# The first forty microseconds of a fused Fourier-and-mixer kernel written anew: other load order, other table order, other first rows

## The chip, the cores and the metric

The kernel runs on one core of a Trainium2 chip. The metric is the time of one execution on the device in microseconds (us); lower is better. The core has a matrix engine (PE, whose weight loads are shown as PEld), a vector engine (DVE), a scalar engine (ACT), a general engine (POOL) and an engine that mostly issues transfers (SP). Each works through its own list of instructions in order and waits on semaphores for the others. Transfers (DMA) are issued from SP, ACT or POOL and are carried by sixteen shared DMA engines.

## The reference

The input x has 8 batches of 3136 rows and 256 columns.

```python
X = np.fft.fft(x, axis=1)
X = np.fft.fft(X, axis=2)
x = X.real                              # what the mixer gets
xt = x.transpose(0, 2, 1)
h = xt @ U @ V                          # U: 3136 x 32, V: 32 x 3136
u = x + h.transpose(0, 2, 1)
ch = np.maximum(u @ w_ch1, 0.0) @ w_ch2 # 256 -> 1024 -> 256
out = u + ch
```

## The kernel before, in words

**The transform.** The Fourier transform over the rows is made by matrix products with tables of sines and cosines. The rows are folded first, so that symmetric and antisymmetric sums take the place of the rows themselves: x is loaded forward (`xf`, by indirect gathers on POOL, `load_f`) and backward (`xr`, by plain loads on SP, `load_r`; rows that stand alone by `load_0`). DVE makes even and odd sums along the columns (`along_d`, giving `EOF_` and `EOR_`; the two lone columns are copied by `alone` on POOL), then along the rows (`mirror`, giving `EOS`; `half`, giving `GE` and `GO`; `fourth`, giving `GC`). All of these DVE folds are recorded by one helper, line 422, so the profile tells them apart by their output: eor, eof, eos, ge, go, gc. PE multiplies them by the tables `TABE`, `TABO`, `TABS` (te, to, ts in the profile; `seq` and `even_rows`, output pt, all PE work through the helper at line 427). Results become `A` and `B`, halves of a spectrum over the rows, through copies on ACT and through `join` and `mirrored` on DVE. A second product with small column tables (`chan`, output pst) gives `S` and `T`, the rows that the mixer needs. A batch's `S` and `T` come in four pieces of 392 or 393 rows, each for S and for T.

**The low-rank part.** U goes through the same transform once, at the start (`transform_u`, output pu, line 295). Its result is written into spare columns of the tables, so that later products deliver the low-rank part along with the transform. `even_k` makes the even half, `odd_k` the odd half, `evict` copies both on ACT. For batch 0 the low-rank part is computed by itself (`u_alone`).

**The mixer.** 12,544 rows (half of each batch; the other half follows from symmetry) are worked through in 25 chunks of 512. `front(c, hf)` adds the low-rank part and stores `u`, then starts a transposing transfer `ut<-u` on SP. `direct` (p<-u,w) is the first mixer product of the direct half. `mirrors` adds a correction in place to get the mirrored half: p<-uo,wd with `WD`, the difference of the two halves of w_ch1, and p<-dv,qf with `DV`, differences of V. ACT applies the relu to both (h, lines 733 and 749). `second_product` (p<-w,h) multiplies by w_ch2, DVE adds `ut` (o, lines 792 and 793), POOL corrects two columns (`fx`), SP stores.

**What sets the order.** Everything up to `second_product(0, 0, 0)` is written out by hand in program order; each engine runs its share in that order. From there a loop over chunks places the later batches' transforms in slots (`due`, `put`, `spread_out`). Batch 1's folds are among the first of these slots; part of them stands in the hand-written beginning.

**The beginning.** The angles are made on DVE (`phase`), the tables on ACT (`sines`, `cosine_odd`, `other_odd` for odd-numbered tables; `sines`, `mirror_even`, `cosine_even`, `halve`, `other_even` for even ones). `negatives` are four small copies for U. `filler` issues products on PE whose result is not used. PSUM is shared by three tags: dft (two buffers), p1 (four) and p2 (two).

Places that matter: `VV` is V, loaded by POOL (line 904) and copied to three further groups of partitions by SP (line 939). `vv` gets one more column at line 960, `DV` is made at line 961, `WD` at 962, all three on DVE, and one row of `WD` is cleared on POOL. W2 is loaded on POOL at line 945, behind the gathers of batch 1's second half of `xf`.

Of the kernel before, what the change touches and what calls it, by code (L numbers as in the profile page):

```python
# [31 lines left out]
def kernel(  # L32
# [47 lines left out]

    def load_0(t, dst_f, dst_r, b, w):

        lo = t.offset + b * S * w
        nc.sync.dma_start(out=dst_f[PQ:KP],
                          in_=bass.AP(t.tensor, lo + (NI - 1) * w,
                                      [[w, 1], [784 * w, 4], [-w, NI], [1, w]]))
        nc.sync.dma_start(out=dst_r[PQ:KP, 0:3].rearrange("p q i d -> p q (i d)"),
                          in_=bass.AP(t.tensor, lo + 784 * w, [[w, 1], [784 * w, 3], [1, NI * w]]))
        nc.sync.dma_start(out=dst_r[PQ:KP, 3].rearrange("p i d -> p (i d)"),
                          in_=bass.AP(t.tensor, lo, [[w, 1], [1, NI * w]]))  # L90
# [35 lines left out]
    krow = gen.tile([P, 4 * NT], FP32, name="krow")  # L126
    kev = gen.tile([P, 2 * NT], FP32, name="kev")
    ncol = cpool.tile([P, NI], FP32, name="ncol")

    def iota(out_, pattern, base, m=0):  # L130
# [70 lines left out]
    def phase(y, a_ap, col_ap, bits):  # L201
# [3 lines left out]
        nc.vector.tensor_single_scalar(y, y, 2 ** bits - 1, op=AL.bitwise_and)  # L205

    def sine(out_, y, bits, sgn):
# [58 lines left out]
    hw = cpool.tile([P, 1], FP32, name="hw")  # L266
    nc.vector.tensor_scalar(hv[:], ncol[:, NI - 1:NI], 0.0, -0.5, op0=AL.is_equal, op1=AL.mult)
    nc.vector.tensor_scalar(hw[:], ncol[:, NI - 1:NI], 0.1245, -0.5, op0=AL.is_gt, op1=AL.mult)
    nc.vector.scalar_tensor_tensor(hv[:], hv[:], 1.0, hw[:], op0=AL.add, op1=AL.add)
    def kp(i):  # L270
# [19 lines left out]
    def transform_u(t, fill=None):  # L290
# [22 lines left out]
        def even_k():  # L313
            pu = PU[t] = psum.tile([P, 16, R], FP32, tag="p2", name="pu", bufs=2)
            for c, i in enumerate((3, 1)):
                for io in range(NI):
                    dst = pu[:kp(io), 2 * io + c, :]
                    if io % 2 == 0:
                        group(dst, [(wo(t, i, io, nm), go(i, nm)) for nm in range(2)])
                    else:  # L320
                        group(dst, [(we(t, i, io), gc(i, io))])
                fill(1)

        def odd_k():
            pu = PU[t]
            for nm in range(2):
                u = 1 - t if nm else t
                for io in (0, 2):
                    group(pu[:PQ, 8 + 2 * nm + io // 2, :],
                          [(wo(u, i, io, nn), go(i, nn, nm == 1 and (i == 2) == (nn == 0)))  # L330
                           for nn in range(2) for i in (0, 2)])
                for io in (1, 3):
                    group(pu[:kp(io), 12 + 2 * nm + io // 2, :],
                          [(we(u, i, io), gc(i, io, nm == 1 and i == 2)) for i in (0, 2)])
                fill(1)

# [59 lines left out]
    def alone(qs, src, dst, eng=None):  # L396

        (eng or nc.gpsimd.tensor_copy)(dst[:, qs, :, 128:257:128], src[:, qs, :, 0:129:128])
# [207 lines left out]
    def chan(b, ch, h, tag="dft"):  # L606
        d = ST[b]
        at, n0 = ((0, 0), (785, 1), (393, 786), (1177, 785))[ch]
        n = 393 if ch == 0 else 392
        pt = psum.tile([P, TE], FP32, tag=tag, name="pst", bufs=BUFS[tag])  # L610
# [22 lines left out]

    def transposed(b):

        pt = psum.tile([P, 2, P], FP32, tag="p2", name="ptd", bufs=BUFS["p2"])
# [4 lines left out]
        nc.scalar.copy(TD[b % 2][:], pt[:])  # L641

    def hidden(b, hh):

        pt = psum.tile([P, CH], FP32, tag="dft", name="pq", bufs=BUFS["dft"])
# [226 lines left out]
    for t in range(2):  # L872
        halve(t)
    for t in range(2):
        other_even(t)
    negatives()

    def filler(tag="dft"):
        pt = psum.tile([P, 2 * NT], FP32, tag=tag, name="fill", bufs=BUFS[tag])

        def some(n):
            for _ in range(n):
                nc.tensor.matmul(pt[:], TABO[0][:PQ, 0, 1, 0:P], TABO[0][:PQ, 0, 0, 0:2 * NT],  # L883
                                 start=True, stop=True)
        return some
# [17 lines left out]
    alone(EV, xf, EOF_)  # L903
    nc.gpsimd.dma_start(out=VV[:R, 0:S], in_=moe_V)
    gather(w1t[:], moe_w_ch1, D, pint[:], H, 0)
    alone(OD, xf, EOF_)
# [74 lines left out]
    mirrored(0, 1, cos_even)  # L981
    odd_part(0)

# [109 lines left out]
```

## Time and profile before

| What | us |
|---|---|
| Median of 3 runs (lowest, highest) | 465.75 (465.24, 467.85) |
| The profiled execution, and its span in the trace | 465.93, 464.1 |
| PE, DVE, ACT, POOL busy | 437.0, 319.3, 296.4, 124.3 |
| First sine on ACT starts | 3.50 |
| First gather of xf on POOL starts | 7.04 |
| First product of U's transform after the even tables | 19.48 |
| Granted TensorE clock at half | 19.15 to 32.80 |
| First channel product of batch 0 (pst) | 37.98 |
| First direct product of chunk 0 (p<-u,w) | 41.50 |
| First p<-dv,qf of chunk 0 | 49.55 |
| First second product (p<-w,h) | 54.89 |

How to read it: the span runs from the first to the last instruction of the one execution that was recorded. The chain of work that ended last is followed back from the last instruction, at each step to what released it. A line of the timeline has the start, the time from the first to the last end, engine, line, operation, output and inputs, and in brackets the idle time ahead and what ended it. A line of windows has the stretch, its length, the busy time (and instructions), the granted clock as a share of full speed, the mean share in which the DMA engines were busy, and GB/s.

### The profile page before, as it was taken

Reading aid. Unit: us, or ns where it says so; the run is one execution under the profiler, and the core shown is the slowest. Engines: PE = TensorE matmul, PEld = TensorE weight load, DVE = VectorE, ACT = ScalarE, POOL = GpSimd, SP = SyncE. Lnnn points to the kernel's source line nnn. Section 1 sums busy time; section 2 is a strip of 40 time slices with the busy share of each in tenths; the row PEclk is TensorE's granted clock in tenths of the full one; section 3 lists DMA queues with packets and bytes.
Section 4 is the critical chain, followed back from the end, with each engine's and each line's share of the span. In section 5 each row is a group of like instructions: output and inputs, shape, how many; then the busy total and the mean of one; then the engine's idle time right before and its main releaser. Section 6 shows DMA issues by size and latency. Waiting matters only on the chain.

```text
span 464.1 us, 8942 instructions
## 1 busy us (share of the span) xinstructions
PE 437.0 (94%) x3267; PEld 288.0 (62%) x3314; DVE 319.3 (69%) x649; ACT 296.4 (64%) x635; POOL 124.3 (27%) x340
## 2 busy tenths in 40 slices
PE   4897898997999999999999999999999999999995
PEld 1584366565756666666766666666666675666674
DVE  8886897787599596677686687768777544443542
ACT  6845655675557665777567756775576755766651
POOL 8651162313123230421233221241133100011010
PEclk9859999999999999999999999999999999999999
DMA  5899399597756947675859368565342532425463
GB/s 145 219 224 203 45 275 140 95 193 158 200 145 168 245 106 183 167 176 148 195 114 239 103 163 131 132 179 150 90 97 69 136 93 54 133 69 160 108 126 111
DMA packets 91231, 68.33 MB, mean 147 GB/s; under 512 B 57470, under 2 KB 84498, under 8 KB 91186
## 3 DMA queue, kind: packets, MB, share of 16 engines
q1 hardware_dynamic: 85714, 53.38, 50.8%
q0 software_dynamic: 5472, 14.36, 12.2%
q8 instruction: 26, 0.43, 0.4%
q14 instruction: 19, 0.16, 0.1%
HBM read 28.86 MB, written 25.69 MB: 118 GB/s over the span
## 4 chain that ended last, share of the span: by engine, by line
PE 82%; DVE 8%; ACT 6%; issue 2%; DMA 1%; DVEq 0%; POOL 0%; POOLq 0%
PE p L427 61%; PE pt L427 10%; PE pst L427 4%; PE ph L427 3%; DVE u L690 2%; PE pq L427 1%; PE pu L295 1%; ACT h L733 1%; PE fill L883 1%; DVE ge L422 1%; PE ptt L427 1%; DVE gc L422 1%; DMA ut<-u 1%; DVE A L582 1%; DVE o L792 1%
## 5 line engine op out<-in xcount | busy, mean ns | idle before, releaser
L427 PE MATMUL p<-w,h 128*128 128x256 bf16 x1576 | 188.6, 273 | 0.0
L427 PEld LDWEIGHTS <-h 128*128 128x128 bf16 x1576 | 149.9, 98 | 39.3 <-issue 16.5
L749 ACT ACTIVATE h<-p 128x512 bf16<-128x512 f32 (+1 forms) x200 | 101.5, 595 | 64.7 <-PE p L427 62.5
L733 ACT ACTIVATE h<-p 128x512 bf16<-128x512 f32 (+1 forms) x200 | 101.8, 601 | 8.9 <-PE p L427 8.8
L792 DVE TENSOR_TENSOR o<-p,ut 128x256 f32<-128x256 f32 x99 | 41.6, 420 | 94.8 <-PE p L427 72.8
L427 PE MATMUL p<-u,w 128*128 128x512 bf16 (+1 forms) x360 | 91.1, 374 | 3.6 <-DVE u L690 0.7
L797 POOL TENSOR_TENSOR o<-o,fx 128x2 f32<-128x2 f32 (+1 forms) x99 | 37.4, 379 | 136.5 <-issue 72.4
L427 PEld LDWEIGHTS <-w 128*128 128x128 bf16 x400 | 39.0, 98 | 40.6 <-issue 2.9
L427 PE MATMUL p<-uo,wd 128*128 128x512 bf16 (+1 forms) x199 | 50.7, 374 | 0.4
L57 POOL DMA_INDIRECT xf<-in_x_dram,xidx x32 | 37.0, 1155 | 18.4 <-issue 6.7
L793 DVE TENSOR_TENSOR o<-p,ut 128x256 f32<-128x256 f32 x99 | 40.9, 413 | 0.0
L422 DVE TENSOR_TENSOR eor<-xr 99x1016 bf16<-99x1016 f32 x32 | 38.3, 1209 | 3.5 <-DMA xr<-in_x_dram 3.5
L422 DVE TENSOR_TENSOR eof<-xf 99x1016 bf16<-99x1016 f32 x32 | 38.2, 1207 | 0.0
L690 DVE TENSOR_TENSOR u<-ph,T 128x512 bf16<-128x512 f32 (+8 forms) x64 | 35.0, 557 | 4.5 <-PE ph L427 2.8
L690 DVE TENSOR_TENSOR u<-ph,S 128x512 bf16<-128x512 f32 (+8 forms) x64 | 35.0, 557 | 1.8 <-PE ph L427 1.3
L706 POOL TENSOR_TENSOR fx<-ut 128x4 f32<-128x4 bf16 x50 | 12.8, 256 | 71.9 <-DMA ut<-u 71.9
L427 PEld LDWEIGHTS <-wd 128*128 128x128 bf16 x200 | 19.5, 97 | 17.1 <-issue 1.0
L427 PE MATMUL pt<-te,gc 98*128 98x229 bf16 (+1 forms) x192 | 24.6, 265 | 3.8 <-DVE u L690 3.6
L705 POOL TENSOR_TENSOR fx<-ut 128x4 f32<-128x4 bf16 x25 | 7.7, 306 | 75.3 <-DMA ut<-u 70.2
L427 PEld LDWEIGHTS <-go 98*128 98x128 bf16 x216 | 20.2, 101 | 8.8 <-issue 2.3
L427 PEld LDWEIGHTS <-gc 98*128 98x128 bf16 x216 | 19.9, 99 | 8.3 <-issue 4.0
L618 ACT CAST T<-pst 128x392 bf16<-128x392 f32 (+1 forms) x28 | 17.4, 621 | 11.5 <-PE pst L427 11.5
(154 smaller groups left out, 468.6 us busy)
## 6 DMA issues: line engine op xcount, KB each, us to landing
out_dram<-o SPq DMA_DIRECT2D x33, 512.0 KB
xr<-in_x_dram SPq DMA_DIRECT2D x14, 784.0 KB
out_dram<-o SPq DMA_DIRECT2D x8, 384.0 KB
out_dram<-o SPq DMA_DIRECT2D x9, 256.0 KB
xr<-in_x_dram SPq DMA_DIRECT2D x1, 1568.0 KB
out_dram<-o SPq DMA_DIRECT2D x8, 128.0 KB
ut<-u SPq DMA_TRANSPOSE x50
vv<-vv SPq DMA_DIRECT2D x3, 196.0 KB
```

Of the source, the lines that this page charges most:

```text
L57: nc.gpsimd.indirect_dma_start(out_, None, bass.AP(t.tensor, t.offset, [[w, rows], [1, w]]), bass.IndirectOffsetOnAxis(idx, 0), element_of ...
L422: ins = nc.vector.tensor_tensor(*a, **k)
L427: ins = nc.tensor.matmul(*a, **k)
L618: nc.scalar.copy(to, pt[:, :n])
L690: nc.vector.tensor_tensor(u[:, s, at:at + hi - lo], phs[s][:, at:at + hi - lo], src, op=AL.add)
L705: nc.gpsimd.tensor_tensor(fx[:, :, 0], ut[:, n:2 * n, 0], ut[:, 0:n, 0], op=AL.subtract)
L706: nc.gpsimd.tensor_tensor(fx[:, :, 1], ut[:, 0:n, 0] if hf else ut[:, n:2 * n, 0], ut[:, n + 1:2 * n + 1, 0], op=AL.subtract)
L733: nc.scalar.activation(k["h", 0][q][:, j - 4 * q, :w], p1[:, :w], AF.Relu)
L749: nc.scalar.activation(k["h", 1][q][:, g, :w], k["p1"][g][:, :w][:, ::-1], AF.Relu)
L792: nc.vector.tensor_tensor(o[:, ts, 0:P], p2[:, :w, 0:P], ut[:rows, ts, 0:P], op=AL.add)
L793: nc.vector.tensor_tensor(o[:, ts, P:D], p2[:, :w, P:D], strip(ut[:rows], (CH // P + t0 + 1) * P, [[P, w], [-1, P]]), op=AL.add)
L797: nc.gpsimd.tensor_tensor(o[:, ts, cols], o[:, ts, cols], fx[:rows, ts, 1 - hf:], op=AL.add)
```

## The change

- **Loads.** The three row loads of U are issued from ACT. On SP, `xr`'s odd half goes ahead of the row loads of x, the even half behind them. The four gathers of batch 0's `xf` move ahead of the clearing of the GO and GC buffers (`zeros`) on POOL, which goes behind the table code.
- **Tables.** `kev` is gone; the even angles are read from parts of `krow` in two instructions instead of one. The odd tables of both kinds are finished before the even ones begin; `negatives` moves ahead of the even cosines. The factor `hv` is made on POOL instead of DVE, with four instructions for three.
- **U's transform.** Both odd halves run first, then the even halves, then the copies. 24 fillers stand ahead, 12 between, 8 behind, where 40 stood ahead; `odd_k` has two fillers where it had one.
- **V and the weights.** V's load and the gather of w1t move ahead on POOL. W2's load moves ahead of the second half of batch 1's gathers. `WD`, the extra column of `VV` and `DV` are made on POOL.
- **Chunk 0's rows.** `first_rows` makes only the first 256 columns of pieces 0 and 1, and later the other 136. Piece 2 takes one more row (393), which piece 1 gave before. `transposed` and the two `hidden` products share one p2 buffer with fillers (`spare`), and pieces of batch 0's last rows use p2.
- **Order around chunk 0.** `odd_part(0)` goes ahead of the last `mirrored`; piece 3 moves behind `direct(0, 1)`; the folds of batch 1's backward rows move: the odd ones behind `front(0, 1)` and behind piece 3, the even ones behind `front(1, 0)`.

```diff
-    load_0(moe_U, UA, UR, 0, R)
+    load_0(moe_U, UA, UR, 0, R, nc.scalar)
     load_r(moe_U, UR, 0, 0, 4, R)
+    load_r(x, xr, 0, 1, 2, D)
     load_0(x, xf, xr, 0, D)
-    for q0 in (1, 0):
-        load_r(x, xr, 0, q0, 2, D)
+    load_r(x, xr, 0, 0, 2, D)
     iota(jv[:], [[1, KP]], 0, 1)
-    iota(kev[:, 0:NT], [[-2, 2], [-4, NT // 2]], 392)
-    iota(kev[:, NT:2 * NT], [[-2, NT]], 391)
+    for q in (0, 2, 1, 3):
+        load_f(x, xf, 0, q, D)
...
-    zeros(nc.gpsimd, 0)
-    zeros(nc.gpsimd, 1)
-    for q in (0, 2, 1, 3):
-        load_f(x, xf, 0, q, D)
...
+    def first_rows(b, at, tag):
+        d = ST[b]
+        n = 256 if at == 0 else 136
+        for h in range(2):
+            pt = psum.tile([P, 2, 256], FP32, tag=tag, name="psf", bufs=BUFS[tag])
+            for c, lo in enumerate((at, 785 + at)):
+                mm(pt[:, c, :n], MC[:, h * P:(h + 1) * P], d["A"][:, lo:lo + n], start=True, stop=False)
+                mm(pt[:, c, :n], MSN[:, h * P:(h + 1) * P], d["B"][:, lo:lo + n], start=False, stop=True)
+            to = strip(d["ST"[h]][:], 2 * at, [[1, 2], [2, n]])
+            if h == 1:
+                nc.vector.tensor_copy(to, pt[:, :, :n])
+            else:
+                nc.scalar.copy(to, pt[:, :, :n])
...
     flipped = flip_u()
-    for i in (3, 1):
-        phase(phe[:, i // 2], kev[:KP], ncol[:KP, i:i + 1], 15)
-        sines(i)
-        mirror_even(0, i)
-    fold_u(flipped)
-    for i in (3, 1):
-        cosine_even(i)
     for i in (0, 2):
         cosine_odd(i)
     for t in range(2):
         other_odd(t)
+    for i in (3, 1):
+        phase_even(i)
+        sines(i)
+        mirror_even(0, i)
+    fold_u(flipped)
+    negatives()
+    for i in (3, 1):
+        cosine_even(i)
+    halves()
+    zeros(nc.gpsimd, 0)
+    zeros(nc.gpsimd, 1)
     for t in range(2):
         halve(t)
     for t in range(2):
         other_even(t)
-    negatives()
...
     alone(OD, xr, EOR_)
+    nc.gpsimd.dma_start(out=VV[:R, 0:S], in_=moe_V)
+    gather(w1t[:], moe_w_ch1, D, pint[:], H, 0)
     alone(EV, xr, EOR_)
...
-    fill(40)
+    fill(24)
     us, uc = transform_u(0, fill), transform_u(1, fill)
-    for f in us + uc:
-        f()
+    us[1]()
+    uc[1]()
+    fill(12)
+    us[0]()
+    uc[0]()
+    us[2]()
+    uc[2]()
+    fill(8)
...
+    nc.gpsimd.dma_start(out=W2[:], in_=moe_w_ch2.rearrange("(j p) d -> p j d", p=P))
     for q in (1, 3):
         load_f(x, xf, 1, q, D)
-    nc.gpsimd.dma_start(out=W2[:], in_=moe_w_ch2.rearrange("(j p) d -> p j d", p=P))
...
     apart(0, 1, sin_odd)
+    nc.gpsimd.tensor_tensor(WD[:], W1[:, 1, :], W1[:, 0, :], op=AL.subtract)
+    nc.gpsimd.memset(WD[0:1], 0.0)
     nc.gpsimd.memset(DV[:, 0:1], 0.0)
-    nc.vector.tensor_copy(VV[2 * R:, S:S + 1], VV[2 * R:, HALF:HALF + 1])
-    nc.vector.tensor_tensor(DV[:, 1:], VV[:, S - 1:HALF:-1], VV[:, 1:HALF], op=AL.subtract)
-    nc.vector.tensor_tensor(WD[:], W1[:, 1, :], W1[:, 0, :], op=AL.subtract)
-    nc.gpsimd.memset(WD[0:1], 0.0)
+    nc.gpsimd.tensor_copy(VV[2 * R:, S:S + 1], VV[2 * R:, HALF:HALF + 1])
+    nc.gpsimd.tensor_tensor(DV[:, 1:], VV[:, S - 1:HALF:-1], VV[:, 1:HALF], op=AL.subtract)
...
-    join(0, 1, 0, sin_odd)
+    join(0, 1, 0, sin_odd, high=False)
     lowrank(0)
-    filler("p2")(6)
-    for ch in range(2):
-        for h in range(2):
-            chan(0, ch, h)
+    spare = psum.tile([P, CH], FP32, tag="p2", name="spare", bufs=BUFS["p2"])
+    transposed(0, spare)
+    filler("p2", spare)(6)
+    join(0, 1, 0, sin_odd, low=False)
+    first_rows(0, 0, "dft")
+    hidden(0, 0, spare)
...
-    alone(OD, xr, EOR_)
-    alone(EV, xr, EOR_)
     front(0, 0)
     mirrored(0, 0, sin_even)
     join(0, 1, 1, cos_odd, low=False)
+    odd_part(0)
     mirrored(0, 1, cos_even)
-    odd_part(0)
...
     direct(0, 0)
-    transposed(0)
-    along_d(OD, xr, EOR_, 0)
     chan(0, 2, 0)
     chan(0, 2, 1)
-    along_d(OD, xr, EOR_, 1)
-    hidden(0, 0)
-    hidden(0, 1)
-    chan(0, 3, 0)
-    chan(0, 3, 1)
+    hidden(0, 1, spare)
+    first_rows(0, 256, "p2")
     mirrors(0, 0)
     front(0, 1)
+    alone(OD, xr, EOR_)
+    along_d(OD, xr, EOR_, 0)
     direct(0, 1)
-    along_d(EV, xr, EOR_, 0)
-    mirrors(0, 1)
-    along_d(EV, xr, EOR_, 1)
-    front(1, 0)
+    chan(0, 3, 0, "p2")
+    chan(0, 3, 1, "p2")
+    along_d(OD, xr, EOR_, 1)
+    mirrors(0, 1)
+    front(1, 0)
+    alone(EV, xr, EOR_)
+    along_d(EV, xr, EOR_, 0)
+    along_d(EV, xr, EOR_, 1)
```

More of the change, by code (lines that the diff above doesn't have):

```diff
@@ L126 @@
     krow = gen.tile([P, 4 * NT], FP32, name="krow")
-    kev = gen.tile([P, 2 * NT], FP32, name="kev")
     ncol = cpool.tile([P, NI], FP32, name="ncol")
@@ L205, in phase, with phase_even @@
         nc.vector.tensor_single_scalar(y, y, 2 ** bits - 1, op=AL.bitwise_and)
+    def phase_even(i):
+        y, col = phe[:, i // 2], ncol[:KP, i:i + 1]
+        for part, src in ((slice(0, NT), strip(krow[:KP], NT // 2, [[NT, 2], [1, NT // 2]])),
+                          (slice(NT, 2 * NT), krow[:KP, 3 * NT:4 * NT])):
+            dst = y[:, part].bitcast(FP32)
+            if part.start == 0:
+                dst = dst.rearrange("p (a j) -> p a j", a=2)
+            nc.vector.tensor_scalar(dst, src, col, float(2 ** (23 - 15)), op0=AL.mult, op1=AL.add)
+        nc.vector.tensor_single_scalar(y, y, 2 ** 15 - 1, op=AL.bitwise_and)
     def sine(out_, y, bits, sgn):
@@ L266, with halves @@
     hw = cpool.tile([P, 1], FP32, name="hw")
-    nc.vector.tensor_scalar(hv[:], ncol[:, NI - 1:NI], 0.0, -0.5, op0=AL.is_equal, op1=AL.mult)
-    nc.vector.tensor_scalar(hw[:], ncol[:, NI - 1:NI], 0.1245, -0.5, op0=AL.is_gt, op1=AL.mult)
-    nc.vector.scalar_tensor_tensor(hv[:], hv[:], 1.0, hw[:], op0=AL.add, op1=AL.add)
+    def halves():
+        nc.gpsimd.tensor_scalar(hv[:], ncol[:, NI - 1:NI], 0.0, -0.5, op0=AL.is_equal, op1=AL.mult)
+        nc.gpsimd.tensor_scalar(hw[:], ncol[:, NI - 1:NI], 0.1245, -0.5, op0=AL.is_gt, op1=AL.mult)
+        nc.gpsimd.tensor_tensor(hv[:], hv[:], hw[:], op=AL.add)
+        nc.gpsimd.tensor_single_scalar(hv[:], hv[:], 1.0, op=AL.add)
     def kp(i):
@@ L313, in even_k @@
         def even_k():
-            pu = PU[t] = psum.tile([P, 16, R], FP32, tag="p2", name="pu", bufs=2)
+            pu = PU[t]
             for c, i in enumerate((3, 1)):
@@ L324, in odd_k @@
         def odd_k():
-            pu = PU[t]
+            pu = PU[t] = psum.tile([P, 16, R], FP32, tag="p2", name="pu", bufs=2)
             for nm in range(2):
@@ L334, in odd_k @@
                           [(we(u, i, io), gc(i, io, nm == 1 and i == 2)) for i in (0, 2)])
-                fill(1)
+                fill(2)
         def evict():
@@ L609, in chan @@
         n = 393 if ch == 0 else 392
+        if b == 0 and ch == 2:
+            at, n0, n = 392, 784, 393
         pt = psum.tile([P, TE], FP32, tag=tag, name="pst", bufs=BUFS[tag])
@@ L632, in lowrank, with transposed @@
         nc.sync.dma_start_transpose(out=TD[b % 2][:], in_=TX[:])
-    def transposed(b):
-        pt = psum.tile([P, 2, P], FP32, tag="p2", name="ptd", bufs=BUFS["p2"])
+    def first_rows(b, at, tag):
[11 more added lines that the diff above has]
+                nc.scalar.copy(to, pt[:, :, :n])
+    def transposed(b, spare):
+        pt = spare[:, 0:2 * P].rearrange("p (s m) -> p s m", s=2)
         for s in range(2):
@@ L640, in transposed, with hidden @@
                    stop=(typ == 1))
-        nc.scalar.copy(TD[b % 2][:], pt[:])
-    def hidden(b, hh):
-        pt = psum.tile([P, CH], FP32, tag="dft", name="pq", bufs=BUFS["dft"])
+        nc.scalar.copy(TD[b % 2][:], pt)
+    def hidden(b, hh, spare=None):
+        pt = spare or psum.tile([P, CH], FP32, tag="dft", name="pq", bufs=BUFS["dft"])
         for s in range(2):
@@ L875, with filler @@
         other_even(t)
-    negatives()
-    def filler(tag="dft"):
-        pt = psum.tile([P, 2 * NT], FP32, tag=tag, name="fill", bufs=BUFS[tag])
+    def filler(tag="dft", pt=None):
+        pt = pt or psum.tile([P, 2 * NT], FP32, tag=tag, name="fill", bufs=BUFS[tag])
         def some(n):
             for _ in range(n):
-                nc.tensor.matmul(pt[:], TABO[0][:PQ, 0, 1, 0:P], TABO[0][:PQ, 0, 0, 0:2 * NT],
+                nc.tensor.matmul(pt[:, 0:2 * NT], TABO[0][:PQ, 0, 1, 0:P], TABO[0][:PQ, 0, 0, 0:2 * NT],
                                  start=True, stop=True)
@@ L903 @@
     alone(EV, xf, EOF_)
-    nc.gpsimd.dma_start(out=VV[:R, 0:S], in_=moe_V)
-    gather(w1t[:], moe_w_ch1, D, pint[:], H, 0)
     alone(OD, xf, EOF_)
```

9 lines of the change are left out of this document (5 added, 4 removed).

## The prediction

> **What bounds the kernel now.** I read the page's slices first, then the clock by its windows, then the chain that ended last, then DVE's rows and the DMA queues of the first 72 us.
>
> ```profile
> PE   4897898997999999999999999999999999999995
> DVE  8886897787599596677686687768777544443542
> PEclk9859999999999999999999999999999999999999
> PE 82%; DVE 8%; ACT 6%; issue 2%; DMA 1%; DVEq 0%; POOL 0%; POOLq 0%
> ```
>
> A slice is 11.6 us. From about slice 6 on PE is at 9 nearly everywhere, and 82% of the chain is PE. The change leaves that stretch's work as it is, so what counts is when PE gets into it: the first second product (p<-w,h) starts at 54.89 us in the timeline. All before it is the beginning, in which slice 3 shows the clock at 5. In stretches of 3.41 us (columns: length, PE busy, granted clock, DMA share, GB/s):
>
> ```profile
> 15.73:19.15 3.42, 1.79 (x11) 1.00 0.84 219
> 19.15:22.56 3.41, 3.08 (x30) 0.50 0.60 124
> 29.39:32.80 3.41, 3.41 (x16) 0.50 1.02 250
> 32.80:36.21 3.41, 3.41 (x70) 1.00 1.03 234
> 43.04:46.45 3.41, 2.21 (x14) 1.00 1.43 138
> ```
>
> After a stretch of which PE was busy 1.79 us the clock halves, and it is whole again after a stretch full of long matmuls. A stretch with 2.21 us keeps it. The half-speed time covers U's transform and the first half of batch 0's.
>
> Between 55 and 71 us the chain runs through DVE, not PE:
>
> ```profile
> 56.31 3.15 DMA ut<-u
> 59.73 0.27 POOL eof L398
> 60.64 0.42 DVE o L792
> ...
> 68.04 1.14 DVE ge L422
> 69.43 1.30 DVE gc L422 x2
> 70.73 0.61 DVE u L690
> 71.38 0.56 PE pt L427 x4
> ```
>
> Here PE waits 1.1 us for DVE's u. So two dates decide: when DVE enters this list, and what the list holds. From 71.4 us to 98.9 us the chain is PE again, so a shift at 71.4 us is taken to the end.
>
> ```profile
> 50.93 0.68 DVE L690 TENSOR_TENSOR u<-ph,S 128x511 bf16<-128x511 f32 x1
> 51.52 2.33 DVE L422 TENSOR_TENSOR eor<-xr 99x1016 bf16<-99x1016 f32 x2
> 54.99 0.69 DVE L690 TENSOR_TENSOR u<-ph,S 128x512 bf16<-128x512 f32 x1 [1.13 <-PE ph L427]
> 60.02 0.70 DVE L422 TENSOR_TENSOR eos<-eof,eor 99x1040 bf16<-99x1040 bf16 x1 [0.55 <-POOL eof L398]
> ```
>
> The eor pair lies in a gap in which DVE waits for chunk 0's second direct product, and 1.13 us are still left over.
>
> **Part by part.**
>
> *Loads first.* In the timeline the first gather of xf starts at 7.04 us, behind memsets from 3.60 to 6.81, and xr's large loads at 5.63, behind three small ones. Now the gathers follow the iotas (about 2.6 us) and xr's odd half goes third (about 2). The row loads of U go to ACT's queue, where ACT sat idle until 3.50 (three issues of 0.42 to 0.82 fit; at worst its first sine is 0.5 us late). The x loads end about 2.5 us earlier, at 16.3 instead of 18.8. DVE's 1.52 us wait for xr at 14.85 goes. The memsets move behind the gathers and end near 12.6, before POOL's first cast, which stood at 12.30.
>
> *Tables.* hv leaves DVE (0.15 + 0.14 + 0.16); the even phases take three instructions for two, twice (+0.35). ACT's list keeps its length, so the even tables stay near 19.5 us, but the odd ones are ready near 11 (16.69 before). The odd half of U's transform then stands where PE had only fillers, and fillers cover the rest up to 19.5. I take the clock as whole from here on: the gap left before batch 0's first products is about 1.3 us, and gaps up to 1.11 us (at 70.27) did no harm, one of 1.9 us (17.6 to 19.5) did. At half speed this stage costs at most 3 us, but not at the end (below).
>
> *DVE up to the first rows.* Less 1.52 and 0.45, plus 0.35: the last quarter-length fold ends at 29.6 us, not 31.22. vv, dv and wd (0.15 + 0.98 + 0.68) and the 1.01 us wait for vv leave DVE, and the second eh waits no longer (0.99), since PE, no longer at half speed, is ahead of it. B's first half is then ready at 32.05 (37.32 before) and the channel products start at 32.6, not 37.98.
>
> *First rows alone.* Two pieces of 256 columns per half instead of two of 393 let the first direct product start after one round of evictions (0.60 on ACT and DVE beside each other) instead of two: 35.1 us instead of 41.50 with the above. The rest of chunk 0's rows, the two pq products and B's and A's mirrored halves (0.60 each on DVE, between) bring PE to mirrors(0,0)'s dv products at 40.5 us, against 49.55.
>
> *dv on POOL.* This decides. In the built program POOL's copy into VV, which stands ahead of the dv subtraction, first waits for the landing of all of batch 1's gathers of xf. On DVE it waited for VV's copies only. Before, the last two gathers start at 29.21 and 30.97:
>
> ```profile
> L57 POOL DMA_INDIRECT xf<-in_x_dram,xidx x2: 1457/1539/1621, 29.2 to 31.0; - x2
> DMA to landing us min/median/max: 12.9/12.9/12.9
> ```
>
> That is 42.1 to 43.9 us. Now W2's load (512 KB) is ahead of them on the same queue, so they are its last entry, as W2 was, whose packets end near 46.5. The queues are full from about 26 us to there (the DMA share is 1.02 to 1.22 in the stretches I read), so the end moves with the end of the x loads, by 2.5, to 44.0. Chunk 0's transposes, which took the DMA share to 2.30 at 44 us, now fall before that end: +0.5. I take 44.5; from 41 (the gathers keep their 12.9 us from 27.5 and 29) to 47 (the transposes cost 3).
>
> Then POOL's copy (0.2) and dv, 1567 columns with two inputs. No POOL row of that size exists. DVE takes 0.98 for it, the floor. POOL's one-row memset of 1024 bf16 took 0.94, so 1567 make 1.44 for one stream and 4.3 for three. [...] dv is there at 44.5 + 0.2 + 2.9 = 47.6 us: 1.95 earlier than 49.55, where PE could have had 9.05. If POOL is late, PE waits behind dv with front(0,1) and all after it, ACT with the second relu, and DVE with u.
>
> [...]
>
> *DVE's list behind dv.* The eor folds of batch 1's odd rows now follow u of front(0,1), with the S and T copies of the last channel piece between; they fill the gap that the even pair filled, and pass it by 0.4. The even pair (2.33) moves behind u of front(1,0), so it lies on the chain; it covers the 0.55 wait for POOL's eof. Net +0.4 + 2.33 - 0.55 = +2.2. Its cast (alone) and the transposes (3.15) are done in its shade.
>
> *The clock once more.* From 40.5 to 47.6 PE has nothing: over 3.4 us, so the clock halves, and front(0,1), eight direct products (0.22 each, then 0.43) and the correction run slow for one stretch or two. ACT's relus (0.51 each) hide part: eight at 0.43 are 3.4 against four relus of 0.51, 2.1. I take +1.0, from 0 to 1.7.
>
> *Free.* Banks: the spare tile shares ptd, fillers and both pq products; its order of writers is PE's own, and a conflict would cost an eviction (0.60) in a stretch where PE is early anyway. W2 earlier: its user stands at 52 us or later. Fewer early fillers: PE is idle otherwise. Queue order on SP is otherwise kept.
>
> **Sum.** -1.95 + 2.2 + 1.0 = +1.25 us. The profiled execution took 465.93 us (span 464.1), so 467.2; it lies 0.18 above the median of the runs, 465.75, so I predict 467.0.
>
> **Rivals.**
>
> *The gathers land early.* If they are down by 37 us, dv is ready at 40.5 and costs nothing. No clock loss: -9.05 + 2.2 = -6.8, 459 us. For it: every load starts earlier, and full overlap of POOL's wait was gained already at 37. Against: the queues have no free share before 46. Landings between give the times between; from 42 us on the gain is under 2.3. Chance of a time below 463.4 this way: 0.28.
>
> *The gathers land late.* With W2's small packets and the transposes both ahead, 47 us, and dv at 4.3: 51.5 us, that is +1.95 + 2.2 + 1.7 = +5.9, 471.6 us. It decides from a landing of about 45.5 on. For it: the last packets before trickled until 48. Chance 0.30.
>
> *The clock stays at half speed from 19 us.* The fillers between the small products might not count as busy: with one filler per six products in 19.15 to 32.80 the clock did not come back. Then the channel products start 3 us later and dv's turn on PE is 43.5: still before 47.6, so alone 467 stands; it only takes away the early landing's gain. Inside the other cases.
>
> *Forecast,* landing at 42 to 45.5: 463.4 to 468.1 us, chance 0.42.
>
> **Numbers.** A change within 0.5% (2.3 us) counts as none; the three runs spread by 2.6. Faster 0.28 (early landing), same 0.42, slower 0.30 (late). The range for 8 in 10 is 459.5 to 470.5; the likeliest case alone has 464 to 468.
>
> **What would show it.** In the trace after: POOL idle from about 34.5 us until the gathers land, then vv and dv of about 3 us; PE idle ahead of p<-dv near 47 us with POOL as releaser; the granted clock 1.00 from 12 to 40 us and 0.50 once behind 44; the first direct product near 35 us; DVE's even eor pair behind the third pair of u. I am wrong if p<-dv follows p<-uo at once near 40 us, if POOL's dv is far from 3 us, or if PE no longer waits for DVE near 71 us.

## The result, and the profile after

The changed kernel takes 468.13 us (median of 17 runs, 464.67 to 474.5), the kernel before 464.5 (17 runs beside it, 462.76 to 467.91). The ratio is 1.0064, with a 95% interval of 1.0036 to 1.0091: 3.0 us slower (1.7 to 4.2), against a forecast of 1.25. The ratio leaves out two executions of the changed kernel that were over 1.5% above its fastest. The profiled execution took 467.82 us with a span of 466.0, which is 1.9 over the one before.

What the new beginning was to give did not come: U's odd half runs early, but batch 0's rows come later than before. The dates, in us:

| | before | after | forecast |
|---|---|---|---|
| xr's even half is down | 16.37 | 19.52 | 14.85 or earlier |
| first product of U's transform | 17.55 | 12.34 | near 11 |
| first channel product | 37.98 | 40.38 | 32.6 |
| first direct product | 41.50 | 42.96 | 35.1 |
| PE is through p<-uo,wd, next is p<-dv | 49.5 | 48.5 | 40.5 |
| first p<-dv | 49.55 | 49.54 | 47.6 |
| batch 1's first pt | 71.38 | 74.62 | |

DVE's timeline after (start, length, engine, line, operation; in brackets the idle time ahead and what ended it) shows where it begins:

```profile
11.38 2.36 DVE L434 TENSOR_TENSOR eor<-xr 99x1016 bf16<-99x1016 f32 x2
19.52 2.35 DVE L434 TENSOR_TENSOR eor<-xr 99x1016 bf16<-99x1016 f32 x2 [5.79 <-DMA xr<-in_x_dram]
```

The wait for xr that was to go has grown from 1.52 to 5.79 us. The load was issued at 4.44 us, not 6.0, and landed 3.1 us later. The DMA queues show what the load shared the engines with (packets, MB, share of the sixteen engines). From 9 to 10 us SP's queue had the engines to itself before:

```profile
q1 hardware_dynamic: 79, 0.28, 87.0%
```

and it shares them with POOL's gathers after:

```profile
q0 software_dynamic: 42, 0.14, 61.4%
q1 hardware_dynamic: 27, 0.11, 47.1%
```

It is so in each microsecond from 7 to 13, with 46.4 to 61.4% for POOL's queue and 31.7 to 49.4% for SP's. DVE needs xr first and xf only behind it, so half of what moved was not yet wanted. POOL's timeline after:

```profile
36.07 2.12 POOL L997 TENSOR_TENSOR wd<-w 128x1024 bf16<-128x1024 bf16 x1
...
46.35 0.18 POOL L1000 COPY vv<-vv 64x1 bf16<-64x1 bf16 x1 [7.12 <-DMA xf<-in_x_dram,xidx]
46.61 2.87 POOL L1001 TENSOR_TENSOR dv<-vv 128x1567 bf16<-128x1567 bf16 x1
```

The copy waits for batch 1's gathers and dv takes 2.87 us, as forecast. PE's timeline after:

```profile
28.71 1.47 PE L439 MATMUL pt<-ts,go 98*128 98x196 bf16 x8 [6.51 <-DVE go L434]
...
47.51 1.03 PE L439 MATMUL p<-uo,wd 128*128 128x512 bf16 x4
49.54 0.40 PE L439 MATMUL p<-dv,qf 32*128 32x512 bf16 x4 [1.00 <-POOL ut L730]
...
63.42 2.76 PE L439 MATMUL p<-w,h 128*128 128x256 bf16 x16 [1.75 <-DVE o L822]
65.98 2.77 PE L439 MATMUL p<-u,w 128*128 128x512 bf16 x8
...
74.62 0.56 PE L439 MATMUL pt<-te,gc 98*128 98x229 bf16 x4 [0.88 <-DVE u L719]
```

Up to the first p<-dv nothing is lost against before (49.54 to 49.55). All of the loss at 74.62, 3.24 us, lies behind it: 1.75 us in which PE waits for o, and the products after it, which take 2.76 us where they took 1.91. The windows after (length, PE busy, PEld, DVE, ACT, POOL, granted clock, DMA share, GB/s) show the clock halve behind that wait:

```profile
60.91:64.32 3.41, 1.66 (x16) 0.93 (x16) 3.25 (x8) 2.06 (x4) 2.93 (x6) 1.00 0.83 233
64.32:67.74 3.42, 3.42 (x15) 1.83 (x13) 3.42 (x6) 0.60 (x1) 1.68 (x5) 0.50 0.96 259
```

In one such stretch at half speed 1.71 us of work are lost. With the wait of 1.75, and 0.23 saved ahead of pt (0.88 for 1.11), that is the 3.24. In DVE's list o stands behind the folds:

```profile
56.31 2.33 DVE L434 TENSOR_TENSOR eor<-xr 99x1016 bf16<-99x1016 f32 x2
...
62.00 0.70 DVE L434 TENSOR_TENSOR eos<-eof,eor 99x1040 bf16<-99x1040 bf16 x1 [0.15 <-POOL eof L410]
62.62 0.42 DVE L821 TENSOR_TENSOR o<-p,ut 128x256 f32<-128x256 f32 x1
```

eos started at 60.02 before: the moved even pair costs 2.0 us here. Behind batch 1's pt some of it comes back, since the wait ahead of batch 2's first pt shrinks. PE's timeline before, and after:

```profile
112.74 0.56 PE L427 MATMUL pt<-te,gc 98*128 98x229 bf16 x4 [2.46 <-DVE u L690]
```

```profile
114.05 0.56 PE L439 MATMUL pt<-te,gc 98*128 98x229 bf16 x4 [0.53 <-DVE u L719]
```

These are 1.31 us apart.

### The profile page after: what moved, and what is told of

Its sections match the earlier page's. It is cut to its first block, busy times and chain, and to the rows that moved or that the text cites. A ratio compares the mean times of both kernels' runs of the same rounds, so it can differ in the third digit from the quotient of the medians.

```text
span 466.0 us, 9026 instructions
## 1 busy us (share of the span) xinstructions
PE 438.0 (94%) x3330; PEld 286.5 (61%) x3330; DVE 317.9 (68%) x645; ACT 296.1 (64%) x635; POOL 126.9 (27%) x345
## 4 chain that ended last, share of the span: by engine, by line
PE 75%; DMA 8%; DVE 7%; issue 4%; ACT 2%; POOL 1%; SPq 1%; POOLq 0%; DVEq 0%
PE p L439 59%; PE pt L439 9%; PE pst L439 3%; DMA xr<-in_x_dram 3%; DMA ut<-u 3%; PE ph L439 2%; DMA out_dram<-o 1%; DVE u L719 1%; PE pq L439 1%; DMA xf<-in_x_dram,xidx 1%; DVE eof L434 1%; DVE gc L434 1%; DVE eor L434 1%; DVE ge L434 1%; DVE A L594 1%
## 5 line engine op out<-in xcount | busy, mean ns | idle before, releaser
L439 PE MATMUL p<-u,w 128*128 128x512 bf16 (+1 forms) x400 | 94.1, 377 | 1.0 <-DVE u L719 0.6
L826 POOL TENSOR_TENSOR o<-o,fx 128x2 f32<-128x2 f32 (+1 forms) x99 | 35.2, 357 | 117.4 <-issue 57.5
L735 POOL TENSOR_TENSOR fx<-ut 128x4 f32<-128x4 bf16 x50 | 16.2, 325 | 77.0 <-DMA ut<-u 76.9
L734 POOL TENSOR_TENSOR fx<-ut 128x4 f32<-128x4 bf16 x25 | 6.7, 269 | 83.8 <-DMA ut<-u 83.8
L439 PEld LDWEIGHTS <-wd 128*128 128x128 bf16 x200 | 19.5, 97 | 16.2
```

The lines of the kernel that those rows point to most:

```text
L439: ins = nc.tensor.matmul(*a, **k)
L734: nc.gpsimd.tensor_tensor(fx[:, :, 0], ut[:, n:2 * n, 0], ut[:, 0:n, 0], op=AL.subtract)
L735: nc.gpsimd.tensor_tensor(fx[:, :, 1], ut[:, 0:n, 0] if hf else ut[:, n:2 * n, 0], ut[:, n + 1:2 * n + 1, 0], op=AL.subtract)
L826: nc.gpsimd.tensor_tensor(o[:, ts, cols], o[:, ts, cols], fx[:rows, ts, 1 - hf:], op=AL.add)
```

## The experiments

Two theories stood against each other. The first: two limits in series hold the front, xr's landing (early gathers) and POOL's dv (landing of batch 1), and only with both gone does it move. The second: the fold order behind dv is the loss, and the front does not matter. All ratios are to the kernel before, run beside; 0.1% is 0.46 us. Single executions of one kernel spread by up to 10 us. A part of that is a wait of PE for DVE's uo at 119 to 125 us, which some profiled executions have and some have not. From batch 2's first pt to batch 3's it is 51.0 to 53.1 us in the profiled executions of the first four experiments, and 46.9 to 47.4 in all others, the kernel before (46.88) and the changed one (46.89) among them. So these four executions hold 4 to 6 us that arise behind 112 us, and what the four say of the front is read from dates. How many executions without a profile have the wait is not known. In each of the four, DVE's o waits 5.6 to 6.7 us there for the store of an earlier o, against 1.98 before and 1.46 after; what makes that store late was not asked.

### Batch 1's folds where they were

```diff
     direct(0, 0)
+    along_d(OD, xr, EOR_, 0)
     chan(0, 2, 0)
     chan(0, 2, 1)
+    along_d(OD, xr, EOR_, 1)
...
     front(0, 1)
     alone(OD, xr, EOR_)
-    along_d(OD, xr, EOR_, 0)
+    alone(EV, xr, EOR_)
+    along_d(EV, xr, EOR_, 0)
...
-    along_d(OD, xr, EOR_, 1)
+    along_d(EV, xr, EOR_, 1)
     mirrors(0, 1)
     front(1, 0)
-    alone(EV, xr, EOR_)
-    along_d(EV, xr, EOR_, 0)
-    along_d(EV, xr, EOR_, 1)
```

> The changed kernel with one part undone: batch 1's four backward folds stand again where they stood before (odd pair behind the first direct product and behind piece 2, even pair behind the second pair of u); their two one-column casts stay behind front(0,1). Theory (the fold order is the loss): the dv products stay near 49.5 us, eos leaves DVE at 60.0 instead of 62.0, PE's 1.75 us wait for o ahead of the second p<-w,h goes, batch 1's first pt moves from 74.6 to about 71.5, and the whole from 3.0 above the kernel before to 0.5 above or less. Rival (the beginning's late loads or POOL's dv are the loss): pt stays at 74 or later and the time stays 2 to 3 us above.

Ratio 1.0134 (1.0081 to 1.0188), 3.3 us above the changed kernel by the two ratios: neither theory had that. DVE's timeline of this kernel:

```profile
46.01 3.68 DVE L434 TENSOR_TENSOR eor<-xr 99x1016 bf16<-99x1016 f32 x1
...
61.24 0.70 DVE L434 TENSOR_TENSOR eos<-eof,eor 99x1040 bf16<-99x1040 bf16 x1 [2.30 <-POOL eof L410]
```

and POOL's:

```profile
45.73 2.88 POOL L1001 TENSOR_TENSOR dv<-vv 128x1567 bf16<-128x1567 bf16 x1
...
60.82 0.20 POOL L735 TENSOR_TENSOR fx<-ut 128x4 f32<-128x4 bf16 x1 [5.61 <-DMA ut<-u]
60.96 0.40 POOL L410 CAST eof<-xf 99x16 bf16<-99x16 f32 x2
```

The list of DVE is free for the second eos from 58.9 us, but it waits for a cast on POOL that stands behind fx, and fx for the transposed rows ut, down at 60.8. So DVE's fold order and POOL's order each hold o near 62 us; undoing one shows the other, and PE's wait for o stays (1.88 us). The first lines show a second thing: an odd fold of 1.20 us takes 3.68 beside POOL's dv and ends at 49.69, 1.1 us behind dv's end, as if nearly all of it was done after dv. Batch 1's first pt is at 72.60, 2.0 us sooner than in the changed kernel, yet this execution is longer (span 468.4): PE waits 2.47 us for uo at 119.33 and runs at half clock behind it, from 119.2 to 122.6 us. That is the later wait named above.

### The gathers late again

```diff
-    for q in (0, 2, 1, 3):
-        load_f(x, xf, 0, q, D)
     lrow = gen.tile([P, 2, P], FP32, name="lrow")
...
+    zeros(nc.gpsimd, 0)
+    zeros(nc.gpsimd, 1)
+    for q in (0, 2, 1, 3):
+        load_f(x, xf, 0, q, D)
     pho = gen.tile([KP, 2, 4 * NT], I32, name="pho", bufs=1)
...
     halves()
-    zeros(nc.gpsimd, 0)
-    zeros(nc.gpsimd, 1)
```

> The changed kernel with one part undone: the GO and GC buffers are cleared ahead of batch 0's four gathers again, so the gathers start near 7 us instead of 2.4. Theory (the early gathers take half the DMA engines from xr's even half): xr lands near 16.4 instead of 19.5, DVE's wait for it falls from 5.8 us to under 2, everything on DVE up to batch 1's gathers is 2.5 to 3 us earlier, and so is dv: p<-dv at 46.5 to 47.5 instead of 49.5. The time falls by 1 to 2.5 us against the changed kernel, to between 0.5 and 2 above the kernel before. Rival (xr's landing is set by its own queue's order or size): xr lands at 18 or later all the same and nothing moves. Second rival (batch 1's landing is fixed by the volume ahead of it): xr lands early, but p<-dv stays within 0.5 us of 49.5 and the time with it.

Ratio 1.0147 (1.0100 to 1.0195): slower still. But DVE has all four eor folds without a wait:

```profile
12.02 4.59 DVE L436 TENSOR_TENSOR eor<-xr 99x1016 bf16<-99x1016 f32 x4
```

The clock stays whole from 12 to 43 us, the first channel product is at 33.31 and the first direct one at 35.89. That is the front of the prediction, to within 1 us. PE's timeline then shows what it is worth:

```profile
40.45 1.03 PE L441 MATMUL p<-uo,wd 128*128 128x512 bf16 x4
49.02 0.61 PE L441 MATMUL p<-dv,qf 32*128 32x512 bf16 x4 [7.54 <-POOL ut L732]
```

PE waits 7.54 us for dv, and p<-dv is nearly where it was (49.02 for 49.54). The clock is halved from 43.9 to 54.1 us, and from p<-dv to the first p<-w,h takes 7.01 us (49.02 to 56.03) for 5.33 in the changed kernel. So the late xr had hidden the wait for dv; the second rival of this run (p<-dv within 0.5 us of 49.5) was right about the dates. The last gather of batch 1 was issued at 29.08 us, 5.07 earlier than in the changed kernel, but took 16.4 us to land instead of 11.9, so it was down only 0.6 us earlier. The front does not explain why this kernel is slower still: at batch 1's first pt it is 0.38 us behind the changed kernel (75.00 and 74.62), at batch 2's 2.20. The largest loss comes behind that, with a wait of 3.59 us for uo at 124.67 and half clock from 125.8 to 129.2 us.

### dv on DVE again

```diff
-    nc.gpsimd.tensor_tensor(WD[:], W1[:, 1, :], W1[:, 0, :], op=AL.subtract)
-    nc.gpsimd.memset(WD[0:1], 0.0)
     nc.gpsimd.memset(DV[:, 0:1], 0.0)
-    nc.gpsimd.tensor_copy(VV[2 * R:, S:S + 1], VV[2 * R:, HALF:HALF + 1])
-    nc.gpsimd.tensor_tensor(DV[:, 1:], VV[:, S - 1:HALF:-1], VV[:, 1:HALF], op=AL.subtract)
+    nc.vector.tensor_copy(VV[2 * R:, S:S + 1], VV[2 * R:, HALF:HALF + 1])
+    nc.vector.tensor_tensor(DV[:, 1:], VV[:, S - 1:HALF:-1], VV[:, 1:HALF], op=AL.subtract)
+    nc.vector.tensor_tensor(WD[:], W1[:, 1, :], W1[:, 0, :], op=AL.subtract)
+    nc.gpsimd.memset(WD[0:1], 0.0)
```

> The changed kernel with one part undone: VV's last column, DV and WD are made on DVE as before, so nothing behind them waits for batch 1's gathers. Theory (dv costs PE 1.0 us and POOL's two-input work also slows DVE): PE goes from p<-uo,wd to p<-dv without a wait, near 48.5 or up to 1 us sooner since the 1.95 us eh of DVE falls back to 0.36 but 1.8 us of dv, wd and the copy come in; the time falls by 0.5 to 2 against the changed kernel. Rival (dv is no loss, only the fold order): p<-dv comes earlier, but DVE's eos stays near 62, and the time stays 2.5 to 3 above the kernel before.

Ratio 1.0065 (1.0022 to 1.0108), as the changed kernel. p<-dv is at 47.90 without a wait and batch 1's pt at 71.72, 2.9 us ahead of the changed kernel. eos starts at 60.37, so the rival put the loss in the wrong place, though the time is where it had it. The twelve times fall into two groups, six from 465.14 to 466.28 and six from 469.61 to 472.08. The profiled execution (470.9) is of the second, and its PE timeline has this line:

```profile
119.92 1.04 PE L439 MATMUL p<-uo,wd 128*128 128x512 bf16 x4 [2.54 <-DVE uo L742]
```

DVE makes this uo behind an o that had waited 5.67 us, and the clock is halved from 121.1 to 124.5 us. That the other group lacks this wait is likely, but no execution of it was profiled: it is inferred.

### Only the copy on DVE

```diff
-    nc.gpsimd.tensor_copy(VV[2 * R:, S:S + 1], VV[2 * R:, HALF:HALF + 1])
+    nc.vector.tensor_copy(VV[2 * R:, S:S + 1], VV[2 * R:, HALF:HALF + 1])
```

> The changed kernel, but with the one-column copy into VV on DVE, while DV and WD stay on POOL: this takes away only the wait of POOL's copy for the landing of batch 1's gathers. Theory (the landing, not POOL's own 2.9 us, is what dates dv): POOL's dv starts behind wd near 39.5 us and is done by 42.5, p<-dv follows p<-uo,wd at once near 48.5, and the time is as with all three on DVE, within 0.7 us. Rival (POOL's slow subtraction is the cost): DVE's instructions beside dv stretch from under 0.6 to 1.5 us or more, and the channel products come 1 to 3 us later than in the changed kernel, so p<-dv is no earlier than 49.5.

Ratio 1.0036 (0.9996 to 1.0076). POOL's dv starts at 39.54 instead of 46.61 and p<-dv follows p<-uo at 48.89. So POOL's wait came from this one instruction of 0.18 us. The profiled execution is the longest of the twelve (472.00); its clock fell early, told of below, and it has the late wait (3.32 us at 120.55). Against the run with all three on DVE the time can't be told apart.

### Both limits undone

The edits of the second and third experiment together.

> The changed kernel with two parts undone: GO and GC cleared ahead of the gathers, and VV's last column, DV and WD on DVE. With the gathers alone undone PE was at p<-uo,wd at 40.45 us and then waited 7.54 us for POOL's dv. Theory (two limits in series, xr's landing and POOL's wait for batch 1's gathers; taking one away shows the other): now p<-dv follows p<-uo,wd at once near 41 to 42.5, 7 us ahead of the changed kernel, the first p<-w,h comes at 47 to 49 instead of 54.9, and the next limit is batch 1's data: DVE's eof and eor wait for landings near 46, so of the 7 us 3 to 5 are left at batch 1's first pt, 68 to 71 us; the time is 1 to 4 us under the changed kernel. Rival (the beginning's dates do not matter, later waits near 62 and 120 us set the time): pt of batch 1 stays at 72 or later, and the time is at 467 or above.

Ratio 0.9949 (0.9915 to 0.9984): 2.4 us under the kernel before, 5.3 under the changed one. PE's timeline:

```profile
42.09 1.03 PE L441 MATMUL p<-uo,wd 128*128 128x512 bf16 x4
43.05 0.40 PE L441 MATMUL p<-dv,qf 32*128 32x512 bf16 x4
...
56.94 1.92 PE L441 MATMUL p<-w,h 128*128 128x256 bf16 x16 [1.75 <-DVE o L824]
...
66.87 0.56 PE L441 MATMUL pt<-te,gc 98*128 98x229 bf16 x4 [1.28 <-DVE u L721]
```

p<-dv is at 49.02 with the one edit, at 47.90 with the other, and at 43.05 with both (49.54 in the changed kernel). That is what two limits in series do; the second theory falls. The times agree (+6.8 us and +3.0 with one edit, -2.4 with both), but in the first two the late wait has a part. The profiled execution here is the shortest of the twelve (460.35, median 463.81). Batch 1's data, which was expected to be the next limit, was not: pt is at 66.87, not 68 to 71. The 1.75 us wait for o has moved along.

### Both undone, and the folds where they were

> As the run with the gathers late and dv on DVE, and batch 1's backward folds in the places of before as well. If the fold order still costs its two microseconds when nothing waits for dv, PE's wait for o ahead of the second chunk's p<-w,h is 1.5 us or more shorter than without it and the time another 1 to 2 us lower: a kernel that beats both, at 461 to 464 us. Rival (xr of batch 1 has not landed when the odd folds now stand in DVE's list, near 36 us): DVE waits up to 9 us for xr ahead of the copies of S and T, PE waits behind them for u, and the time is 2 us or more above the run without this edit.

Ratio 0.9955 (0.9917 to 0.9993), no difference, and from p<-dv to batch 1's pt it is 23.87 us for 23.82. DVE waits 1.58 us for xr of batch 1 at 42.05, and PE still waits 1.72 us for o: eos stands at 56.11 behind a wait of 1.97 us for POOL's eof. It is the wait of the first experiment.

### And the cast ahead of fx

```diff
     mirrors(0, 1)
+    alone(EV, xf, EOF_)
     front(1, 0)
...
-            yield lambda qf=qf: (alone(qf, xf, EOF_), along_d(qf, xf, EOF_, 0))
+            yield lambda qf=qf, nm=nm: ((b == 1 and nm == 0) or alone(qf, xf, EOF_), along_d(qf, xf, EOF_, 0))
```

> As the run with gathers late, dv on DVE and folds as before, with one more edit: POOL's two-column cast of batch 1's even forward rows (eof) stands ahead of the third pair of u, so it no longer queues behind POOL's fx, which waits for the transposed rows ut. Theory (with the fold order restored, PE's 1.72 us wait for o near 57.5 us is POOL's order: fx waits for ut's landing at 55.7, eof's cast for fx, eos for the cast, o for eos): eos leaves DVE at about 54.8 instead of 56.8, the wait for o goes or falls under 0.5, and batch 1's pt moves from 67.5 to 66 to 67; the time falls by 0 to 1.7 us. Rival (DVE's own list sets eos and o): the wait stays above 1.2 us and pt at 67.5.

Ratio 0.9890 (0.9838 to 0.9942): 5.1 us under the kernel before, median 461.39. It is faster than the kernel before and than the changed one; against the run without the cast's move the intervals overlap. POOL's timeline of this kernel:

```profile
48.13 0.26 POOL L412 CAST eof<-xf 99x16 bf16<-99x16 f32 x1
...
53.73 0.20 POOL L737 TENSOR_TENSOR fx<-ut 128x4 f32<-128x4 bf16 x1 [5.33 <-DMA ut<-u]
```

and PE's:

```profile
53.57 1.92 PE L441 MATMUL p<-w,h 128*128 128x256 bf16 x16
...
63.21 0.56 PE L441 MATMUL pt<-te,gc 98*128 98x229 bf16 x4 [1.00 <-DVE u L721]
```

The cast is done before fx's wait of 5.33 us, and p<-w,h has no wait for o. From the first p<-dv to pt it is 21.86 us (63.21 - 41.35), 23.87 without the edit (67.52 - 43.65): 2.0 us. The front of this execution is 2.3 us earlier than that of the run before it too, with the same instructions up to there (first pt of batch 0 at 23.59 and 25.88), so the edit itself is worth about 2 of the 4.3 us at pt. Which of the parts of the change that are left (tables, U's transform, first rows) gives how much of the 5.1 us was not tried.

### The loads alone, on the kernel before

```diff
-    load_0(moe_U, UA, UR, 0, R)
+    load_0(moe_U, UA, UR, 0, R, nc.scalar)
     load_r(moe_U, UR, 0, 0, 4, R)
+    load_r(x, xr, 0, 1, 2, D)
     load_0(x, xf, xr, 0, D)
-    for q0 in (1, 0):
-        load_r(x, xr, 0, q0, 2, D)
+    load_r(x, xr, 0, 0, 2, D)
     iota(jv[:], [[1, KP]], 0, 1)
+    for q in (0, 2, 1, 3):
+        load_f(x, xf, 0, q, D)
     iota(kev[:, 0:NT], [[-2, 2], [-4, NT // 2]], 392)
...
     zeros(nc.gpsimd, 1)
-    for q in (0, 2, 1, 3):
-        load_f(x, xf, 0, q, D)
```

> The kernel before with the load part of the change alone: U's row loads on ACT, xr's odd half ahead of the row loads, the four gathers ahead of the clearing of GO and GC. Theory (gathers that start early take half the DMA engines from xr): xr's even half lands near 19 instead of 16.4, DVE's wait for it grows from 1.5 to 4 or 5 us, everything on DVE behind it is 2 to 3 us later, and so is the first second product (57 instead of 54.9); the time is 1.5 to 3.5 us above the kernel before. Rival (the changed table order, not the loads, delays DVE): the wait stays under 2 us and the time within 1 us of the kernel before.

Ratio 1.0086 (1.0057 to 1.0115), 4.0 us slower. xr's even half is down at 18.00 us, 1.6 later than in the kernel before and 1.5 sooner than in the changed one, so the wait (2.04 us) is under the expectation. The dates of the front: first channel product 39.24 (+1.3), batch 1's xr at 47.88 in DVE's list instead of 45.83, half clock from 43.8 to 47.2 us, first p<-w,h 58.03 (+3.1). The load part by itself loses time, but not by xr alone. The gathers stand ahead of `kev` here, which the changed kernel does without. DVE's timeline, and PE's:

```profile
8.22 0.50 DVE L206 TENSOR_SCALAR phe<-kev,ncol 99x392 f32<-99x392 f32 x1 [3.07 <-POOL kev L132]
```

```profile
21.16 0.26 PE L296 MATMUL pu<-guo,ts 99*98 99x32 bf16 x1 [1.70 <-ACT ts L388]
```

PE starts this product 1.68 us later than before (19.48) and runs without a wait from there to batch 0's first pt (29.32, 27.63 before), at half clock all the way (from 19.9 to 33.6 us). So kev on POOL makes PE late by as much as xr makes DVE late, and this run does not part the two; the run with the gathers late has neither in its way. Whether V's and w1t's loads, which stay late in this kernel, make up the 1.5 us between 18.0 and 19.5 was not tried.

### The gathers late, the copy on DVE

The second and the fourth edit together: POOL is free of the landing but still makes wd and dv.

> The changed kernel with the gathers late and the one-column copy into VV on DVE; DV and WD stay on POOL. Theory (of the 7.54 us that PE waited with the gathers late, all is POOL's wait for the landing, none its speed): POOL's wd and dv run back to back from about 31.5 to 37, p<-dv follows p<-uo at once near 42, within 1 us of the run with dv on DVE, and the time is within 1.5 us of that run. Rival (POOL's two-input subtractions of 2.1 and 2.9 us hold up DVE's folds beside them, as one fold of 1.20 us took 3.68 beside dv): eh, A and B come 2 to 5 us later than with dv on DVE, p<-dv at 44 to 47, the time 2 us or more above that run.

Ratio 0.9982 (0.9947 to 1.0017). wd and dv run from 32.85 to 38.83, p<-dv follows p<-uo at 44.41. The 7.54 us were POOL's wait. POOL's work is not free, though; DVE's timeline, beside a wd of 2.11 us from 32.85:

```profile
32.22 2.96 DVE L537 TENSOR_TENSOR eh<-ev 128x196 f32<-128x196 f32 x1
35.10 0.35 DVE L539 TENSOR_TENSOR eh<-ev 128x196 f32<-128x196 f32 x1
```

The same form takes 2.96 us beside wd and 0.35 behind it. p<-dv is 1.36 us later than with dv on DVE, but batch 0's first pt was already 1.87 later in this execution (25.49 and 23.62), so these two do not price the stall, and the intervals of the two times overlap.

## Why the forecast came out as it did

The time, 468.1 by the median or 465.75 + 3.0 = 468.7 by the ratio, is in the range and at the edge of the likeliest case (464 to 468); the interval of 1.7 to 4.2 us lies across the bound of 2.3 between no change and slower. The sum is near, but several of its terms are not.

*Loads first, wrong.* "The x loads end about 2.5 us earlier" and "DVE's 1.52 us wait for xr at 14.85 goes" took the issue dates for the landing dates. The engines were at 87 to 95% from 8 to 12 us before; moving the gathers forward did not shorten the whole (the last one, issued at 6.50, took 15.7 us to land), it halved what the first-needed load got. In its place stands a wait of 5.79 us. With the gathers late again the wait is gone.

*Tables, right; the clock, wrong.* U's first product came at 12.34 (11). "The gap left before batch 0's first products is about 1.3 us" hung on the step above: it was 6.51, and the clock was at half from 26.8 to 33.6 us. Until PE ran dry at 22 us it was whole, so the rival in which fillers do not count did not come about here. It is not refuted: in the run with only the copy on DVE the clock fell within U's transform, at 17.0 us, and stayed at half until 34.1 although PE had work or fillers without a gap up to 27.9. A small term was off too: "at worst its first sine is 0.5 us late" became 1.08 (4.58 for 3.50), and no harm of it is seen.

*First rows and PE's own path, right without the loads.* 32.6, 35.1 and 40.5 were forecast for the first channel product, the first direct product and the turn of dv; with the gathers late 33.31, 35.89 and 41.48 were measured. In the changed kernel they are 40.38, 42.96 and 48.5.

*dv on POOL, right in mechanism.* Wait for the gathers, copy 0.2 (0.18), dv 2.9 (2.87). No run shows why dv takes 2.9 us rather than 1.44 or 4.3; they show its time, 2.87 or 2.88 in the five runs with dv on POOL, wd's, 2.11 or 2.12 in four of them, and POOL in the changed kernel waiting from 39.2 us, not 34.5. What was mis-sized is the landing: 44.5 forecast, 46.3 measured. So dv was there at 49.48 instead of 47.6, and the term of -1.95 us measured -0.01. By its own mark ("from a landing of about 45.5 on") this was the case of the late rival, without its price for dv (4.3). The step that gave 44.5 was "the end moves with the end of the x loads". The last gathers stand behind DVE's folds and were issued at 32.38 and 34.15, 3.2 us later than before, because xr was late. But that is not the whole: with the gathers late the x loads ended 3.9 us earlier (18.3 for 22.2, the landing of batch 0's last gather), the last gathers of batch 1 were issued 5.07 us earlier, and they were still down only at 45.5 (29.08 + 16.4). So the early landing (0.28) came in no run; what holds it there was not tried, the volume ahead of it on the queues is the rival named for that run.

*DVE's list, right in size.* +2.2 forecast, +2.0 measured at eos. But the step did not follow it to PE's wait for o (1.75 us), nor see that POOL's order behind ut holds o at nearly the same date.

*The clock once more, at the top of its range, and in another place.* "From 40.5 to 47.6 PE has nothing" was 1.00 us in the event, and the clock stayed whole there. It was halved at 64 to 68 us instead, 1.71 us for the forecast 1.0 (0 to 1.7). Within a long wait of PE it did fall in two places: from 43.9 in the 7.54 us with the gathers late, and from 26.78 in the 6.51 us of the changed kernel.

*"A shift at 71.4 us is taken to the end", wrong.* Of 3.24 us at batch 1's pt 1.31 were left at batch 2's, because the wait of 2.46 us there shrank. At the end of the profiled execution it is 1.9.

So -1.95 + 2.2 + 1.0 became -0.01 + 3.25 - 1.93 up to batch 2, and 0.6 more by the end of this execution; the other 1.1 of the 3.0 us by the ratio are not in it. The nearness of the sum is luck: the gain that was to come from the front was nothing, and a part of the loss that was to stay went away.

## What to carry to other kernels

Of a load moved forward, ask whose share of a full DMA it takes: what is needed first should have the engines to itself (SP's queue had 87.0% of them from 9 to 10 us before, 47.1% after), and the issue date says little of the landing (xr's even half was issued at 4.44 us for 6.0 and landed 3.1 us later). Before work is moved to an idle engine, list everything that its first instruction waits for; here a copy of 0.18 us carried a wait of 7 us for data that it does not use. Where two waits end near the same date, undo them together: each alone left p<-dv within 1.7 us of its place, the pair brought it 6.5 us forward. And follow a kernel's loss by dates to the end: here 4 to 6 us of it arose behind 112 us in four of the runs, far from the edits.

## What the runs showed of the hardware

Three of DVE's subtractions took longer beside a subtraction on POOL: an eor 3.68 us for 1.20 beside dv (batch 1's folds where they were), an eh 1.95 for 0.36 beside wd in the changed kernel, and an eh 2.96 for 0.35 with the gathers late and the copy on DVE. The last one's record starts 0.6 us ahead of wd's (32.22 and 32.85), and it was long all the same. DVE's copy T<-psf at 47.71, inside the dv of the changed kernel (46.61 to 49.48), kept its 0.46. What sets the copy apart from the three was not tried. The prediction priced dv and wd by POOL's time alone.

The clock fell after a stretch of 3.41 us with PE busy for 1.66, and in the kernel before after one with 1.79, so no idle stretch was needed. Busy time alone does not decide it, though. Lines of windows, with the columns as above, from the run with dv on DVE:

```profile
59.66:63.08 3.42, 1.67 (x18) 1.17 (x13) 3.27 (x7) 2.06 (x4) 2.94 (x6) 1.00 0.86 229
63.08:66.49 3.41, 3.36 (x25) 2.29 (x25) 3.41 (x7) 2.06 (x4) 1.68 (x5) 1.00 0.99 278
```

and from the run with only the copy on DVE:

```profile
13.62:17.03 3.41, 2.70 (x43) 2.31 (x41) 3.10 (x5) 2.83 (x9) 1.17 (x2) 1.00 1.01 231
17.03:20.44 3.41, 3.41 (x18) 1.83 (x17) 0.56 (x1) 3.31 (x10) 0.53 (x1) 0.50 0.88 183
```

The same wait of 1.75 us for o, whole within one stretch and with PE busy for 1.67, left the clock whole in the first; 2.70 us of small products did not keep it in the second. So the prediction's reading from the kernel before, that a stretch with 2.21 us keeps the clock, does not carry over, and what decides stays open. In the changed kernel the clock fell at 26.78, rose at 33.60 and fell at 64.32: 6.82 and 30.72 us apart, which are two and nine times the 3.41 us of these stretches.
